# Attention and two feed-forward layers on one core: loads kept off the first two rows of maxima, the second copy of Q on ScalarE for two pairs, and another order around them

## The chip, the core and the metric

The kernel runs on one core of a Trainium2 chip. The core has five engines that run on their own and meet at semaphores: TensorE (PE) multiplies matrices, VectorE (DVE), ScalarE (ACT) and GpSimd (POOL) work on elements, and SyncE (SP) issues the DMAs, in the order in which they stand in its queue. The metric is the time of one execution in device microseconds; lower is better. Inputs and outputs lie in the chip's own memory (HBM).

## What is computed

```python
# attention over q, k, v of (4, 8, 576, 64) and s of (4, 8, 576)
scores = q @ k.T / sqrt(64)
cum = np.cumsum(np.maximum(s, 0.0), axis=-1)
scores = np.where(causal, -1e9, scores + np.minimum(cum[..., None, :] - cum[..., :, None], 0.0))
scores = scores - scores.max(-1, keepdims=True)
attn = np.exp(scores); attn = attn / (attn.sum(-1, keepdims=True) + 1e-9)
x = (attn @ v)                       # laid out as (2304, 512)
h = x @ moe_w_in;  x = (h - np.tanh(h)) @ moe_w_out           # 512 -> 2048 -> 512
h = x @ moe2_w_in; out = (h * clip(h + 3, 0, 6) / 6) @ moe2_w_out
```

## The kernel before

There are 32 heads, worked on two at a time as 16 *pairs* (p = 0 to 15). Every product is made of parts, a rounded high part and the rest as a low part, so that it comes out close to full precision. The attention stage runs over the pairs; the two feed-forward layers follow.

The program does not write its order out. It lists operations with an engine, an estimated duration, what they come after, the buffers that they take and a priority (PRIO), and `plan.schedule()` (L193 on) plays them in time: a free engine takes the ready operation of the smallest priority. The order that comes of it is what each engine and SP's queue then run. Afterwards the list MOVES puts four operations elsewhere by hand, and the table FILLS puts idle matmuls of zeros (L1354) on PE ahead of named operations, so many microseconds of them, but none ahead of an operation that stands behind the first pair's `pv`. The first zeros of all (L1369) run while the first loads are on their way.

For a pair these operations are made, by the names of the plan:

- `lq`, `lk` load Q and K of the pair (L490, 288 KB each; the first pair in halves, one per head). `lv` loads V (L598, 330 KB).
- `q1` makes the high part of Q (ACT, L466 and L468) and `kh` that of K (DVE, L477). `k2` is the second copy of the high part of K (ACT, L480), `q2` the second copy of that of Q, a DMA inside the core's memory (L279, `Q<-Q`, 288 KB). `ql` and `kl` are the low parts (POOL, L474 and L484). `cu` brings the cumulated s (L279, `K<-cdram`); it writes into the pair's K buffer, so it waits until the pair four before it has done with that buffer.
- `mx` are five products of high parts for the row maxima alone (PE, L531): `mx2_0` of pair 1 is the wide one, `mx2_1` to `mx2_4` take one bank each. `rd` reduces them (DVE, L540).
- `mf` turns the maxima into a row (DVE, L569 to L576), `mo` writes that row out (L279, `mdram<-xr`, 16 KB), and `mi` reads it back into the pair's Q buffer (L279, `Q<-mdram`). The maxima so enter the next product as one more row of it. `mo` and `mi` of a pair are what is called *a row of maxima under way* here. The first pair has two of them, one per head.
- `st` are the scores of a head in four chunks (PE, L633), `ex` their exponentials (ACT, L636), and `pv` the product with V and the sums of a pair (PE, L666 and L677). A chunk waits for a free PSUM bank; a bank of `mx` is free when its `rd` has read it, a bank of `st` when its `ex` has. `ov` (ACT, L701) empties the banks of `pv`.

Operations are named by the head that ends the pair: `mx4` and `rd4` are of pair 2, `st0` and `st1` of the heads of pair 0, `pv1` of pair 0.

The loads of later pairs wait for rows of maxima by this line, and those of V by the next one:

```python
[cm] if p == 1 else first_mo[:1] if p == 2 else first_mo[1:2] if p else []      # lq, lk
first_mo[1:2] if p else first_mo[:1]                                            # lv
```

`first_mo` is the list of all `mo`, in the order of the pairs, so that `first_mo[0]` and `first_mo[1]` are the two of pair 0.

Of the kernel before, what the change touches and what calls it, by code (L numbers as in the profile page):

```python
# [14 lines left out]
AF = mybir.ActivationFunctionType  # L15
# [17 lines left out]
FILLS = {"mx1_0": 0.9, "mx2_1": 3.0, "st0_0": 0.9, "mx4_1": 2.4, "st1_0": 0.5, "pv1_3": 1.5}  # L33
# [35 lines left out]
KDMA = ()  # L69
TINY, HUGE = (float(np.array([b], np.uint32).view(np.float32)[0]) for b in (0x38000000, 0x47F00000))  # L70
# [9 lines left out]
PRIO = {  # L80
# [3 lines left out]
}  # L84
# [46 lines left out]
class Plan:  # L131
    LAT = {"PE": 0.30, "ACT": 0.05, "DVE": 0.09, "POOL": 0.09, "V": 0.0}
    DMA_US, DMA_KB_US, ISSUE = 1.6, 220.0, 0.55
# [126 lines left out]
def kernel(  # L260
# [10 lines left out]
    nc = tc.nc  # L271
    plan = Plan()
# [43 lines left out]
    def r(b):  # L316
        return late[b.t] if isinstance(b.t, str) else b.t
# [125 lines left out]
    first_mf, first_mo = [], []  # L443
# [6 lines left out]
    def heads(p):  # L450
# [10 lines left out]
        for i, a in enumerate(parts):  # L461
# [26 lines left out]
            def ld(x, a=a):  # L488
                dst = r(tq)[x * D : (x + 1) * D, a].rearrange("p a s -> p (a s)")
                nc.sync.dma_start(dst, (q, k)[x][p][:, a.start * S : a.stop * S])  # L490

            lq, lk = (plan.dma(
                lambda x=x, ld=ld: ld(x), 147 * n, [cm] if p == 1 else first_mo[:1] if p == 2 else first_mo[1:2] if p else [], [tq], t + PRIO["lq"], name=f"l{'qk'[x]}{p}"
# [8 lines left out]
            oq2.append(plan.dma(q2, 147 * n, [oq1[-1], a2], [b1, b2], t + PRIO["q2"], name=f"q2_{p}"))  # L502
# [60 lines left out]
        for i, a in enumerate(parts):  # L563
# [27 lines left out]
            u = t0 + PRIO["mf"] if p else lead + a.start  # L591
# [843 lines left out]
```

## Time and profile before

| | |
|---|---|
| runs of the kernel, us | 947.81, 944.92, 949.15; median 947.81 |
| the profiled execution: its time, us | 944.47 |
| its span in the profile, us | 942.7 |
| PE busy | 931.3 us, 99% |
| DVE / ACT / POOL busy | 662.9 / 467.3 / 159.3 us |

The profile is of one execution of its own. A time counts some 1.8 us more than the span, which runs from the first to the last instruction. PE's busy time includes the matmuls of zeros. Times in the rows below are microseconds from the span's start.

### The profile page before, as it was taken

The page shows a single profiled execution, that of the slowest core. Times are in us where ns is not written, and L with a number is a line of the kernel's source. Part 1 is how long each engine was busy: PE and PEld are TensorE (multiplying, and loading weights), DVE is VectorE, ACT ScalarE, POOL GpSimd, SP SyncE. Part 2 cuts the span into 40 slices and gives each one's busy share as a digit, 9 for nine tenths or more (in the row PEclk, how much of TensorE's full clock was granted, in tenths as well). Part 3 has the DMA queues.
Part 4 walks back from the last instruction along what each step waited for, and adds up shares of the span by engine and source line. Part 5 has one row for each costly group of instructions (what it writes and reads, how often), then busy time and mean ns, then how long its engine had stood idle before and what let it go on. Part 6 is the DMA issues. An engine that isn't in the chain of part 4 may idle for free.

```text
span 942.7 us, 18003 instructions
## 1 busy us (share of the span) xinstructions
PE 931.3 (99%) x7112; PEld 839.0 (89%) x7112; DVE 662.9 (70%) x1059; ACT 467.3 (50%) x720; POOL 159.3 (17%) x113
## 2 busy tenths in 40 slices
PE   8999999999999999999999999999999999999998
PEld 5888888788788889988888888999999999999997
DVE  7798897889985776676577641848767477674763
ACT  7577777655443444444344333544545344454441
POOL 7446756500000000022332321000000000000000
PEclk9999999999999999999999999999999999999999
DMA  5666876777235445564546862766887668776762
GB/s 156 170 180 176 235 197 182 229 286 233 89 121 220 179 185 217 202 202 156 216 153 223 262 218 78 261 214 222 267 276 242 212 221 267 274 245 216 223 223 92
DMA packets 69793, 193.75 MB, mean 206 GB/s; under 512 B 11856, under 2 KB 20656, under 8 KB 68428
## 3 DMA queue, kind: packets, MB, share of 16 engines
q1 hardware_dynamic: 69708, 192.59, 63.0%
q8 instruction: 56, 0.92, 0.4%
q14 instruction: 29, 0.24, 0.1%
HBM read 143.74 MB, written 44.09 MB: 199 GB/s over the span
## 4 chain that ended last, share of the span: by engine, by line
PE 91%; DVE 5%; POOL 1%; DMA 1%; issue 1%; ACT 1%; SPq 0%; DVEq 0%; POOLq 0%; ACTq 0%
PE bank L903 21%; PE bank L934 20%; PE pair L1271 19%; PE pair L1195 18%; PE bank L633 5%; PE bank L666 3%; DVE xr L540 2%; PE bank L677 2%; PE bank L531 1%; PE wide L531 1%; DMA Q<-Q 1%; PE bank L1354 1%; DVE xr L572 1%; DVE K L477 0%; POOL K L484 0%
## 5 line engine op out<-in xcount | busy, mean ns | idle before, releaser
L934 PE MATMUL bank<-gg,w 128*128 128x512 f32 (+1 forms) x960 | 234.4, 368 | 0.5 <-ACT gg L922 0.5
L903 PE MATMUL bank<-xx,w 128*128 128x512 f32 (+1 forms) x960 | 233.4, 368 | 0.0
L934 PEld LDWEIGHTS bank<-gg,w 128*128 128x128 f32 x960 | 170.4, 188 | 30.6 <-ACT gg L922 0.9
L903 PEld LDWEIGHTS bank<-xx,w 128*128 128x128 f32 x960 | 170.4, 189 | 30.2 <-issue 0.2
L1195 PE MATMUL pair<-op_w,w 128*128 128x384 f32 x648 | 117.9, 335 | 0.2
L1195 PEld LDWEIGHTS pair<-op_w,w 128*128 128x128 f32 x648 | 112.4, 188 | 1.2 <-DVE g L918 0.6
L914 ACT ACTIVATE g<-bank 128x512 f32<-128x512 f32 (+1 forms) x80 | 44.4, 555 | 136.9 <-PE bank L903 66.3
L924 POOL TENSOR_TENSOR gg<-g,gg 128x512 fp32r<-128x512 f32 x32 | 48.3, 1510 | 343.8 <-ACT gg L922 246.6
L918 DVE TENSOR_TENSOR g<-bank,g 128x512 f32<-128x512 f32 (+1 forms) x80 | 50.9, 636 | 73.5 <-ACT g L914 72.6
L1271 PE MATMUL pair<-w,op_W 128*128 128x256 f32 x774 | 97.8, 283 | 0.0
L1271 PEld LDWEIGHTS pair<-w,op_W 128*128 128x128 f32 x774 | 95.4, 192 | 0.0
L922 ACT ACTIVATE gg<-g 128x512 fp32r<-128x512 f32 (+1 forms) x80 | 47.0, 588 | 49.4 <-DVE g L918 27.4
L633 PE MATMUL bank<-Q,K 128*128 128x320 f32 (+9 forms) x384 | 65.8, 313 | 1.8 <-DMA Q<-Q 0.9
L636 ACT ACTIVATE pt<-bank 128x512 f32<-128x512 f32 (+2 forms) x128 | 59.1, 508 | 17.1 <-PE bank L633 12.0
L633 PEld LDWEIGHTS bank<-Q,K 128*128 128x128 f32 (+3 forms) x384 | 56.2, 186 | 8.1 <-issue 2.5
L1271 PE MATMUL pair<-w,op_B 128*128 128x256 f32 x486 | 62.7, 283 | 0.0
L1271 PEld LDWEIGHTS pair<-w,op_B 128*128 128x128 f32 x486 | 60.5, 192 | 0.0
L540 DVE CUSTOM_DVE_ANT_0 xr<-bank,xr 128x512 bf16<-128x512 f32 (+3 forms) x96 | 49.0, 510 | 14.5 <-PE bank L531 3.8
L474 POOL TENSOR_TENSOR Q<-tq,Q 64x1152 fp32r<-64x1152 f32 (+1 forms) x17 | 43.0, 2530 | 46.5 <-PE bank L531 22.2
L666 PE MATMUL bank<-pt,vf 128*32 128x192 f32 (+3 forms) x1152 | 46.7, 315 | 0.0
L484 POOL TENSOR_TENSOR K<-tq,K 64x1152 fp32r<-64x1152 f32 (+1 forms) x17 | 42.8, 2522 | 10.9 <-ACT Q L468 3.7
L666 PEld LDWEIGHTS bank<-pt,vf 128*32 128x32 f32 x1152 | 32.1, 110 | 11.0 <-DVE xr L540 0.6
(322 smaller groups left out, 1347.2 us busy)
## 6 DMA issues: line engine op xcount, KB each, us to landing
w<-wdram SPq DMA_DIRECT2D x149, 512.0 KB
wdram<-cv SPq DMA_DIRECT2D x56, 512.0 KB
raw_c<-in_w_dram SPq DMA_DIRECT2D x11, 1024.0 KB
raw_b<-in_w_dram SPq DMA_DIRECT2D x11, 1024.0 KB
raw_a<-in_w_dram SPq DMA_DIRECT2D x12, 512.0 KB
vf<-in_v_dram SPq DMA_DIRECT2D x16, 330.0 KB
rb<-rdram SPq DMA_DIRECT2D x32, 144.0 KB
xdram<-xb SPq DMA_DIRECT2D x16, 288.0 KB
```

Source lines behind the costliest of these rows:

```text
L540: nc.vector.tensor_tensor_reduce(out=junk[0:rr, 0:w], in0=r(b)[0:rr, col : col + w], in1=maskB[:, 0:w] if hh < 0 else maskA[0:rr, m0 : m0 ...
L633: nc.tensor.matmul(o, w, x, start=(i == 0), stop=(i == len(mms) - 1), skip_group_check=True)
L636: nc.scalar.activation(r(pt), r(b)[:, 0 : CW[c]], AF.Exp, scale=0.125)
L666: nc.tensor.matmul(r((wide_b, rest_b)[far])[32 * i : 32 * i + 32, oc : oc + n], r(vf)[:, j, hh, d0 : d0 + 32], r(pts[hh][c])[:, col : col ...
L903: nc.tensor.matmul(r(ps)[:, 0:w], wt[:, c, :], x(c)[:, 0:w], start=(part == 0 and c == 0), stop=(part == 2 and c == NCC - 1),)
L914: nc.scalar.activation(r(g)[:, 0:w], r(ps)[:, 0:w], AF.Tanh)
L918: nc.vector.tensor_sub(x, r(ps)[:, 0:w], x)
L922: gho = plan.op("ACT", vec_us(w, 1.2, 205), lambda: nc.scalar.activation(r(gh)[:, 0:w], r(g)[:, 0:w], AF.Copy), [m, to_gg], [g, gh], base)
L924: glo = plan.op("DVE" if beside else "POOL", vec_us(w, 0.96, 155) if beside else vec_us(w, 0.44, 160), lambda: (nc.vector if beside else n ...
L934: nc.tensor.matmul(r(acc[e])[:, 0:w], a[:, es], bb[:, 0:w], start=f, stop=l)
L1195: nc.tensor.matmul(bank(k)[:, l], w[hw][:, l, kc], r(x)[:, hx, kc], start=(i in (1, 5, 2) and j == 0 and kc == 0), stop=(j == 2 and kc == ...
L1271: nc.tensor.matmul(r(c[k])[:, m * 256 : (m + 1) * 256], r(x)[:, hx, l, m * P : (m + 1) * P], w[hw][:, l], start=(i == order[chain_first[k] ...
```

## The change

Five things are changed.

- `lq2`, `lk2` get a fixed early priority, the loads of Q and K of pair 3 and later wait for `first_mo[2]`, the row of maxima of pair 1, in place of that of pair 0's second head; V of pair 0 waits for that second head's row and V of the later pairs for pair 1's `mi`; `q2` of pair 1 waits for the second row of pair 0 as well.
- For pairs 2 and 3 (QACT) `q2` is no DMA but an ACTIVATE on ACT that reads Q where it was loaded.
- `mf`, `mo` and `mi` of pair 1 get a priority ahead of all else.
- The priorities of the whole attention stage (PRIO) and the assumed DMA rate are other numbers, so the plan comes out in another order.
- FILLS has other lengths and places, and the conversion of the weights may begin after the scores of head 3 in place of head 1.

```diff
-FILLS = {"mx1_0": 0.9, "mx2_1": 3.0, "st0_0": 0.9, "mx4_1": 2.4, "st1_0": 0.5, "pv1_3": 1.5}
+FILLS = {"mx1_0": 0.9, "mx2_1": 4.4, "mx4_1": 1.2, "pv1_3": 0.7, "st3_0": 0.7}
...
+QACT = (2, 3)
...
-    ... "rd": 29.37,
+    ... "rd": 103.23,
...
-                ..., first_mo[:1] if p == 2 else first_mo[1:2] if p else [], [tq], t + PRIO["lq"], ...
+                ..., first_mo[:1] if p == 2 else first_mo[2:3] if p else [], [tq], lead + 2 if p == 2 else t + PRIO["lq"], ...
...
-            oq2.append(plan.dma(q2, 147 * n, [oq1[-1], a2], [b1, b2], t + PRIO["q2"], name=f"q2_{p}"))
+            if p in QACT:
+                oq2.append(plan.op("ACT", act, lambda a=a: nc.scalar.activation(r(b2)[0][0:64, a], r(tq)[0:64, a], AF.Copy), [lq, a2], [b2, tq], t + PRIO["k2"] + 1, name=f"q2_{p}"))
+            else:
+                oq2.append(plan.dma(q2, 147 * n, [oq1[-1], a2] + first_mo[1:2] * (p == 1), [b1, b2], lead + 5 if p == 1 else t + PRIO["q2"], name=f"q2_{p}"))
...
-            u = t0 + PRIO["mf"] if p else lead + a.start
+            u = t0 + PRIO["mf"] if p > 1 else lead + a.start - 100 * p
...
+            first_mi.append(omi[-1])
-        lv = plan.dma(..., first_mo[1:2] if p else first_mo[:1], [vf], t0 + PRIO["lv"], name=f"lv{p}")
+        lv = plan.dma(..., first_mi[2:3] if p else first_mo[1:2], [vf], t0 + PRIO["lv"] if p else lead + 3, name=f"lv{p}")
...
-                fc, [part], PRIO["conv"] + 2 * fc + part, [st_done[1][0]], rawp, wyp)
+                fc, [part], PRIO["conv"] + 2 * fc + part, [st_done[3][0]], rawp, wyp)
```

What it moves is seen at three places. Line numbers of the changed kernel are up to five higher. The first place is SP's queue from the `cu2` load on, before:

```order
L279 DMA K_2_103<-cdram 2x2x576
L279 DMA mdram<-xr 128x32
L279 DMA Q_1_110<-Q_1_99 64x2x576
L598 DMA vf_112<-in_v_dram 128x660
L279 DMA Q_0_96<-mdram 2x20x32
L490 DMA tq<-in_q_dram 64x1152
L490 DMA tq<-in_k_dram 64x1152
L279 DMA K_3_106<-cdram 2x2x576
L279 DMA mdram<-xr 128x32
L598 DMA vf_113<-in_v_dram 128x660
L598 DMA vf_114<-in_v_dram 128x660
L279 DMA Q_0_96<-mdram 2x20x32
```

and the same place now, as far as the loads of pair 3:

```order
L280 DMA mdram<-xr 128x32
L280 DMA Q_0_96<-mdram 2x20x32
L491 DMA tq<-in_q_dram 64x1152
L491 DMA tq<-in_k_dram 64x1152
L280 DMA K_3_106<-cdram 2x2x576
L280 DMA mdram<-xr 128x32
L280 DMA Q_0_96<-mdram 2x20x32
L603 DMA vf_112<-in_v_dram 128x660
L280 DMA Q_1_110<-Q_1_99 64x2x576
L280 DMA mdram<-xr 128x32
L280 DMA K_0_97<-cdram 2x2x576
L280 DMA Q_1_99<-mdram 2x40x32
```

The copy `q2` of pair 1 (`Q_1_110<-Q_1_99`) and `lv0` (`vf_112`) have gone from between `mo` and `mi` of the first head to behind both rows, `lv1` and `lv2` from between `mo` and `mi` of the second head to further back; `lq2` and `lk2` (`tq`) still stand between the first `mi` and the second `mo`. Behind the last row shown come `lq3` and `lk3`, which before stood right behind the twelve rows of before; now `cu4` (`K_0_97`) and the row of pair 1 are ahead of them.

The second place is DVE and ACT around the first head's scores. On DVE the end of `rd2`, before:

```order
L540 ISA xr<-bank_66,xr 128x128
L540 ISA xr 128x1
L540 ISA xr<-wide,xr 128x576
L540 ISA xr 128x1
L540 ISA xr<-wide,xr 128x384
L540 ISA xr 128x1
L569 COPY xr<-xr 64x1
L572 TENSOR_SCALAR xr<-xr 128x10
L573 SCALAR_TENSOR_TENSOR xr<-xr 128x10
L576 STREAM_TRANSPOSE xr<-xr 128x32
L477 CAST K_2_103<-tq 64x2x576
```

and now:

```order
L544 ISA xr<-bank_66,xr 128x128
L544 ISA xr 128x1
L478 CAST K_2_103<-tq 64x2x576
L544 ISA xr<-wide,xr 128x576
L544 ISA xr 128x1
L544 ISA xr<-wide,xr 128x384
L544 ISA xr 128x1
L544 ISA xr<-bank_73,xr 128x512
L544 ISA xr 128x1
L544 ISA xr<-bank_71,xr 128x512
L544 ISA xr 128x1
L573 COPY xr<-xr 64x1
```

`kh2` (the CAST) now stands ahead of the wide reduction, and `mf1` (from the COPY on) behind the first two reductions of pair 2. On ACT from the second exponential of head 1 on, before:

```order
L636 ACTIVATE pt_1_119<-bank_73 128x320
L466 ACTIVATE Q_3_105<-tq 64x2x576
L468 ACTIVATE Q_3_107<-tq 64x64
L636 ACTIVATE pt_1_122<-bank_65 128x512
L636 ACTIVATE pt_1_125<-bank_70 128x512
L480 ACTIVATE K_0_109<-tq 64x2x576
L466 ACTIVATE Q_0_96<-tq 64x2x576
```

and now, from the third on:

```order
L641 ACTIVATE pt_1_122<-bank_73 128x512
L641 ACTIVATE pt_1_125<-bank_71 128x512
L481 ACTIVATE K_0_109<-tq 64x2x576
L504 ACTIVATE Q_0_108<-tq 64x1152
L467 ACTIVATE Q_3_105<-tq 64x2x576
L469 ACTIVATE Q_3_107<-tq 64x64
L641 ACTIVATE pt_2_117<-bank_65 128x256
L641 ACTIVATE pt_2_120<-bank_73 128x320
L706 ACTIVATE stage<-bank_70 128x288
L706 ACTIVATE xb_83<-bank_72 128x384
L641 ACTIVATE pt_2_123<-bank_71 128x512
L706 ACTIVATE xb_83<-bank_70 128x192
```

Before, `q1` of pair 3 (`Q_3_105`, `Q_3_107`) stood ahead of the last two exponentials of head 1. Now it stands behind them and behind the new copy `q2` of pair 2 (L504), and ahead of the first exponential of head 2; `q1` of pair 4 and then the last exponential of head 2, again from bank_71, follow the rows shown.

The third place is PE between the maxima of pair 14 and the scores of head 24, before:

```order
L531 MATMUL bank_65<-K_2_103,Q_2_102 128x384
L531 MATMUL bank_65<-K_2_103,Q_2_102 128x128
L633 MATMUL bank_66<-Q_0_108,K_0_109 128x256
L633 MATMUL bank_66<-Q_0_96,K_0_97 128x256
L633 LDWEIGHTS identb
L633 MATMUL bank_66<-maskT,identb 128x128
L633 MATMUL bank_70<-Q_0_108,K_0_109 128x320
L633 MATMUL bank_70<-Q_0_96,K_0_97 128x320
L666 MATMUL bank_73<-pt_1_116,vf_114 32x256 x2
```

and now:

```order
L535 MATMUL bank_66<-K_2_103,Q_2_102 128x384
L535 MATMUL bank_66<-K_2_103,Q_2_102 128x128
L671 MATMUL bank_71<-pt_1_116,vf_114 32x256 x2
L671 MATMUL bank_71<-pt_2_117,vf_114 32x256 x2
L671 MATMUL bank_71<-pt_1_119,vf_114 32x128 x2
```

The first two chunks of head 24 (`st24_0`, `st24_1`) stood ahead of `pv23` and now stand behind it. On PE at the start the rows of zeros now count 7, 38, 10 and 6 (ahead of `mx1_0`, `mx2_1`, `mx4_1` and `pv1`), before 7, 26, 7, 20, 4 and 13; the entry for `st3_0` puts none in.

## Rows read from the trace of the kernel before

**Rows 1.** The page, busy time of each engine, share of the span, instructions

```profile
PE 931.3 (99%) x7112; PEld 839.0 (89%) x7112; DVE 662.9 (70%) x1059; ACT 467.3 (50%) x720; POOL 159.3 (17%) x113
```

**Rows 2.** Waits of PE from 30.5 us on: in total, times, longest

```profile
PE bank L633 <- DMA Q<-Q: 0.9, 1, 0.9
PE bank L633 <- POOL K L484: 0.8, 1, 0.8
PE bank L934 <- ACT gg L922: 0.5, 1, 0.5
PE wide L531 <- ACT xb L701: 0.4, 1, 0.4
```

**Rows 3.** Timeline of PE: start, duration, what, [idle before, releaser]

```profile
11.27 3.01 PE L1354 MATMUL bank<-xr 128*128 128x256 bf16 x26
15.79 0.70 PE L531 MATMUL bank<-K,Q 66*128 66x512 f32 x2 [1.50 <-DVE K L477]
...
24.76 1.17 PE L531 MATMUL bank<-K,Q 66*128 66x512 f32 x6 [0.48 <-issue]
...
30.56 2.92 PE L666 MATMUL bank<-pt,vf 128*32 128x256 f32 x72
...
34.81 0.73 PE L531 MATMUL bank<-K,Q 66*128 66x512 f32 x2
...
36.72 0.45 PE L633 MATMUL bank<-Q,K 128*128 128x256 f32 x2
...
38.60 0.49 PE L633 MATMUL bank<-Q,K 128*128 128x256 f32 x2
...
42.87 2.92 PE L666 MATMUL bank<-pt,vf 128*32 128x256 f32 x72
```

**Rows 4.** Stretches: busy by engine, PE's granted clock, DMA share, GB/s

```profile
17.40:20.80 3.40, 3.40 (x17) 2.85 (x16) 2.87 (x12) 0.53 (x2) 2.67 (x2) 0.50 0.95 249
```

**Rows 5.** Timeline of DVE

```profile
17.90 0.67 DVE L540 CUSTOM_DVE_ANT_0 xr<-bank,xr 128x512 bf16<-128x512 f32 x1
21.66 0.76 DVE L540 CUSTOM_DVE_ANT_0 xr<-wide,xr 128x576 bf16<-128x576 f32 x1
23.90 0.76 DVE L477 CAST K<-tq 64x1152 fp32r<-64x1152 f32 x1
25.27 0.69 DVE L540 CUSTOM_DVE_ANT_0 xr<-bank,xr 128x512 bf16<-128x512 f32 x1 [0.61 <-PE bank L531]
30.48 0.15 DVE L569 COPY xr<-xr 64x1 f32<-64x1 f32 x1
47.84 0.76 DVE L477 CAST K<-tq 64x1152 fp32r<-64x1152 f32 x1
```

**Rows 6.** Timeline of SP's queue, issues

```profile
9.64 0.59 SPq L490 DMA_DIRECT2D tq<-in_k_dram  x1
...
13.69 0.36 SPq L279 DMA_DIRECT2D mdram<-xr  x1
...
15.53 0.79 SPq L279 DMA_DIRECT2D Q<-mdram  x1
16.95 0.59 SPq L490 DMA_DIRECT2D tq<-in_k_dram  x1
...
29.11 0.25 SPq L279 DMA_DIRECT2D K<-cdram  x1
```

**Rows 7.** Timeline of ACT

```profile
12.53 1.16 ACT L466 ACTIVATE Q<-tq 64x1152 fp32r<-64x1152 f32 x1 [1.19 <-DMA tq<-in_q_dram]
14.17 1.16 ACT L480 ACTIVATE K<-tq 64x1152 fp32r<-64x1152 f32 x1 [0.33 <-DMA tq<-in_k_dram]
28.33 1.15 ACT L466 ACTIVATE Q<-tq 64x1152 fp32r<-64x1152 f32 x1
29.53 1.06 ACT L636 ACTIVATE pt<-bank 128x512 f32<-128x512 f32 x2
```

**Rows 8.** The chain that ended last: start, duration, what

```profile
136.60 8.29 DMA Q<-Q
```

More of the change, by code (lines that the diff above doesn't have):

```diff
@@ L132 @@
     LAT = {"PE": 0.30, "ACT": 0.05, "DVE": 0.09, "POOL": 0.09, "V": 0.0}
-    DMA_US, DMA_KB_US, ISSUE = 1.6, 220.0, 0.55
+    DMA_US, DMA_KB_US, ISSUE = 1.6, 240.0, 0.55
     def __init__(self):
@@ L442 @@
     alloc_prev = [None, None]
-    first_mf, first_mo = [], []
+    first_mf, first_mo, first_mi = [], [], []
     filled = []
@@ L492, in heads @@
             lq, lk = (plan.dma(
-                lambda x=x, ld=ld: ld(x), 147 * n, [cm] if p == 1 else first_mo[:1] if p == 2 else first_mo[1:2] if p else [], [tq], t + PRIO["lq"], name=f"l{'qk'[x]}{p}"
+                lambda x=x, ld=ld: ld(x), 147 * n, [cm] if p == 1 else first_mo[:1] if p == 2 else first_mo[2:3] if p else [], [tq], lead + 2 if p == 2 else t + PRIO["lq"], name=f"l{'qk'[x]}{p}"
             ) for x in range(2))
@@ L596, in heads @@
             omi.append(plan.dma(mi, 5, [omo], [b1], u, name=f"mi{p}"))
-        lv = plan.dma(lambda: nc.sync.dma_start(r(vf).rearrange("p j a d -> p (j a d)"), v[p]), 338, first_mo[1:2] if p else first_mo[:1], [vf], t0 + PRIO["lv"], name=f"lv{p}")
+            first_mi.append(omi[-1])
+        lv = plan.dma(lambda: nc.sync.dma_start(r(vf).rearrange("p j a d -> p (j a d)"), v[p]), 338, first_mi[2:3] if p else first_mo[1:2], [vf], t0 + PRIO["lv"] if p else lead + 3, name=f"lv{p}")
         k2s.append(ok2[-1])
```

6 rows, old and new, of the table PRIO are left out of this document.

## The prediction

> **What bounds the kernel now.** The page comes first [rows 1]: PE is busy for 99% of the span. That figure hides two things. Zeros count as busy, and all 77 of them stand in the first 31 us. So the second view is PE's waits from 30.5 us on [rows 2]: in all that is left PE waits 2.6 us. From the first `pv` on, the kernel is a queue of matmuls without gaps, and a change of order can win there no more than those 2.6 us. What is left to win lies ahead of `pv1` at 30.56 [rows 3].
>
> The third view is PE's timeline up to there [rows 3]. The useful work ahead of `pv1` is five sets of maxima or their halves and two heads. One set takes 1.91 us (34.81 to 36.72) and one head 1.88 us (36.72 to 38.60) at full clock. The rest is zeros and waiting: `mx2` waits 1.50 us for `kh1`, `mx4` begins at 24.76, after 0.48 us of idle, as soon as `kh2` is done (23.90 + 0.76) [rows 3, 5]. So `kh2` on DVE set `mx4`, and `mx4`, `st1` and the exponentials behind it set `pv1`: the last two of head 1 end at 29.53 + 1.06 = 30.59 [rows 7]. The chain through the start is DVE's, not that of the rows of maxima alone.
>
> **The start, step by step.** Zeros ahead of `mx2` go from 26 to 38. 26 take 3.01 us [rows 3], so 38 take 4.40 us and end at 15.67, just as `kh1` is done; the 1.50 us of idle go. Behind that idle the granted clock stood at 0.50 for 3.4 us [rows 4], so `mx2` and the first chunks of `st0` ran at the lower level (1.2 GHz). Now `mx2` ends at 15.79 + 1.91 = 17.7.
>
> `st0` needs the first row. Its `mo` was issued at 13.69, and `mi` at 15.53 did not wait [rows 6], so 1.84 us bound such a small transfer when nothing big is ahead of it; it was the big copies between the two that came ahead of `mi`. Now `mi` is issued at 15.5 and lands by 17.4, and `st0` begins at 17.7, with no zeros ahead of it. Its third chunk takes bank_72, which the first reduction of pair 1 (17.90 + 0.67) frees at 18.7 [rows 5], so `st0` ends at 19.9.
>
> `kh2` moves ahead of the wide reduction, which began at 21.66 [rows 5]: it ends at 22.42 and `mx4` begins at 22.5, 2.25 us sooner. That needs `lk2` by 21.66. `lk1` was issued at 9.64 and awaited at 14.17, 4.53 us [rows 6, 7]; `lk2`, issued at 16.95 as before, lands by 21.5. It is close, but the loads ahead of it have gone. The wide part of `mx4` then waits for the wide reduction (from 22.42 on, some 1.4 us by its 0.76 us for 576 of 960 columns), so `mx4` ends at 24.9 and `st1` at 26.8. The second row still has `lq2` and `lk2` ahead of it; behind 21.5 and twice 1.84 would be 25.2 at the very latest, against a need at 24.9, and since `mo` was issued at 18.1, its own time runs beside theirs. I count it at nothing.
>
> With `q1` of pair 3 (1.15 us and a short one, at 28.33 [rows 7]) gone from between the exponentials, the last one ends 0.8 us behind `st1`, and **`pv1` begins at 27.8 and not at 30.56: -2.75 us.**
>
> **What is given back.** `lq3` and `lk3` now stand behind `cu4` and the row of pair 1. `cu4` was issued at 29.11, when `st1` was done [rows 6]; it now goes at 26.9. `mf1` ends at 26.4 (the two reductions of pair 2 ahead of it and 0.85 us of its own, behind 23.85; 0.85 is what the 2.24 us from 21.66 to 23.90 leave beside the wide reduction [rows 5]), its `mo` takes 1.84 us, `mi` 0.79 us of issue, so `lk3` is issued at 29.65. By `lk1`'s 4.53 us it lands at 34.2; with nothing but `lq3` ahead of it sooner. I take 33.5. `kh3` then ends at 34.25. PE, at 27.8 + 4.25 for `pv1` (30.56 to 34.81) + 1.26 for three chunks of head 2 = 33.3, **waits 1.05 us** for it ahead of `mx6`. Before, this load was long there.
>
> A rule of the Trainium skill bears on this: DMA: Bandwidth & Descriptors, section "Queues, rings and completion order", says that each DMA engine takes its descriptors in the order of its ring. By that rule `lk3` waits for `lq3` alone, 0.59 MB in all at the 249 GB/s of [rows 4], and lands at about 33.0, which would make the sum 0.5 us better.
>
> ACT: `lq1` was there 1.64 us ahead of `lk1` [rows 7], so `lq3` comes at 31.9 and `q1` of pair 3 holds ACT from then to 33.3, ahead of the exponentials of head 2. `q1` of pair 4 stands ahead of the last of these, and `st3`'s third chunk takes the same bank_71: ACT's work from 33.3 on sums to 4.4 us, so that chunk begins at 38.0 and PE **waits 0.5 us**. The two copies on ACT themselves (some 1.16 us each, as `q1`) lie beside `pv1` and `pv3`, where ACT waits for PE anyway; without that cover each would cost as much.
>
> DVE: five reductions take 5.2 us (25.27 to 30.48 [rows 5]). Four of them now stand ahead of `kh4`: from 34.9, when the first product of `mx6` is there, 4.2 us and 0.76 us give 39.9. PE, ready for `mx8` at 39.2, **waits 0.7 us**. So `pv3` begins at 41.85. Before it was 42.87 [rows 3] with a quarter of a head (0.46 us) done that now comes later, 42.41 like for like. **Of 2.75 us, 0.55 us are left.** DVE says the same at `kh5`: 39.9 + 1.0 + 5.2 + two `mf` of 0.85 + 0.76 = 48.6, where before it ended at 47.84 + 0.76 = 48.6 [rows 5]. DVE hardly gains there, and PE's lead is some half microsecond of scores done beforehand.
>
> **Later.** The wait of 0.9 us for `Q<-Q` [rows 2] is the copy `q2` of pair 12: 8.29 us from issue to landing [rows 8]. Its first user, `st24_0`, stood ahead of `pv23` and now stands behind it, 4.25 us later, so **the wait goes: -0.9 us**. Those of 0.8, 0.5 and 0.4 I leave as they are: bounds 0 and twice as long. Converting the weights later costs nothing, since from 190 us on PE has no wait for it in [rows 2] and the last part was done before.
>
> **The sum**: -2.75 + 1.05 + 0.5 + 0.7 = -0.5, and -0.9 from the later wait: -1.5 us with the rounding. The profiled execution takes 944.47 us, so 943.0 for one like it. It lies 3.3 us under the median of the runs, 947.81, and the times to come are of that kind: 946.3.
>
> **Rivals.** *The clock falls again* (chance 0.16). Ten zeros behind `st0` last 1.16 us, to 21.05, and `mx4` comes at 22.5: 1.45 us of idle, where 1.50 us were followed by 3.4 us at 0.50 [rows 3, 4]; the idle of 0.48 was not. Then half of 3.4 us, 1.7 us, is lost in `mx4` and `st1`. The row of pair 1 does not wait for that, so `lk3` is only 0.45 us later and the waits behind it shrink; DVE's `kh4` ends at 40.5, and 0.65 us remain: 947.0. The skill's page TensorE: Matmul & The Clock Gate, Part 1, speaks for it: the array is throttled by default and activity lifts that. By that rule alone the sum would be -0.85.
>
> *DVE takes it all* (0.17). It is the engine that PE waits for at 24.76 and, by time, at 48.6. If it loses the half microsecond too, and another wait takes the place of that at `st24`, nothing is won: 947.8. This is also the case where the change does what it says and it doesn't matter, since rows of maxima were not what PE waited for.
>
> *Slower* (0.13). `lk3` was issued early before and its time was hidden; now it is on the path. If it lands as late as the `Q<-Q` of 8.29 us, at 37.95, `mx6` is 4.45 us later than counted, and the sum is +2.95: 950.8. It decides from 1.5 us on, that is a landing behind 35.0. Against it: that copy had a stretch full of other transfers ahead of it.
>
> *All of it stays* (0.14). `lk3` and ACT are in time and no new wait arises: -2.75 and -0.9, 944.1.
>
> My forecast has 0.40. The range is 943.2 to 950.8: the fast case and 0.9 us more for the other old waits, and the slow case. A measurement of this kernel tells some 0.5%, 4.7 us, from no change, and no case reaches that far alone: faster 0.06, same 0.89, slower 0.05.
>
> **What would show it.** Right: `pv1` at 27 to 28.5 us; PE's clock full from 17 to 21 us; a wait of PE for `kh3` (L478) near 33 us and one ahead of `mx8`; no wait for `Q<-Q` near 145 us; `pv3` within a microsecond of 41.9. Wrong: `pv1` behind 29.5 would mean that `lk2` or the second row was late; a wait of over 3 us at `mx6` the slow rival; no waits between 32 and 42 us the fast one. A change of over 5 us could only come from the feed-forward layers, where I see PE without waits and the same work.

## The result and the profile after

| | before | after |
|---|---|---|
| runs, us: median (lowest to highest) | 947.36 (944.92 to 949.15), 6 runs | 957.27 (952.52 to 964.59), 6 runs |
| ratio of the times, 95% interval | | 1.011 (1.0067 to 1.0155) |
| mean granted clock of PE, six runs of after | | 0.982 to 0.992 |
| profiled execution: time, span, us | 944.47, 942.7 | 964.59, 962.8 |

The changed kernel is about 10 us, 1.1%, slower. The forecast was 946.3 us and the range ended at 950.8: the prediction was wrong. The execution that was profiled is the slowest of the six, so its rows show the loss enlarged.

Of the page, the busy time of each engine in the changed kernel, and then PE's waits from 30.5 us on (in total, times, longest):

```profile
PE 944.6 (98%) x7096; PEld 847.5 (88%) x7096; DVE 661.9 (69%) x1059; ACT 468.7 (49%) x722; POOL 158.1 (16%) x113
```

```profile
PE bank L638 <- DMA Q<-mdram: 2.7, 1, 2.7
PE bank L535 <- ACT xb L706: 2.5, 1, 2.5
PE wide L535 <- DVE K L478: 1.7, 1, 1.7
PE bank L638 <- ACT xb L706: 0.8, 1, 0.8
PE wide L535 <- DVE xr L577: 0.7, 1, 0.7
```

PE is 13.3 us longer busy than in [rows 1] with 16 matmuls of zeros fewer, and its waits have grown from one of 0.9 us [rows 2] to two of over 2.5 us. Longer busy on the same work fits a slower clock, which the stretches below show. PE's timeline of the start:

```profile
22.41 1.17 PE L535 MATMUL bank<-K,Q 66*128 66x512 f32 x6 [1.17 <-ACT pt L641]
...
27.45 2.92 PE L671 MATMUL bank<-pt,vf 128*32 128x256 f32 x72
...
35.79 0.47 PE L535 MATMUL bank<-K,Q 66*128 66x512 f32 x1 [2.55 <-ACT xb L706]
...
46.50 4.86 PE L671 MATMUL bank<-pt,vf 128*32 128x256 f32 x72
```

`pv1` begins at 27.45, 3.1 us sooner than in [rows 3]. Then `mx6` waits 2.55 us, and the next `pv` takes 4.86 us for what took 2.92. The releaser named ahead of `mx6`, the last `xb` of ACT, frees a bank; `kh3` on DVE ended within 0.04 us of it. Timelines of DVE, SP's queue and ACT:

```profile
34.93 0.76 DVE L478 CAST K<-tq 64x1152 fp32r<-64x1152 f32 x1 [4.51 <-DMA tq<-in_k_dram]
```

```profile
26.29 0.32 SPq L280 DMA_DIRECT2D mdram<-xr  x1
26.77 0.25 SPq L280 DMA_DIRECT2D K<-cdram  x1
27.74 0.66 SPq L280 DMA_DIRECT2D Q<-mdram  x1
28.50 0.52 SPq L491 DMA_DIRECT2D tq<-in_q_dram  x1
29.08 0.59 SPq L491 DMA_DIRECT2D tq<-in_k_dram  x1
29.76 0.54 SPq L491 DMA_DIRECT2D tq<-in_q_dram  x1
30.36 1.05 SPq L603 DMA_DIRECT2D vf<-in_v_dram  x2
```

```profile
32.39 1.16 ACT L467 ACTIVATE Q<-tq 64x1152 fp32r<-64x1152 f32 x1 [2.51 <-DMA tq<-in_q_dram]
...
35.32 0.32 ACT L706 ACTIVATE xb<-bank 128x192 f32<-128x192 f32 x1
```

`lk3` was issued at 29.08 behind the row of pair 1, as foreseen, but landed at 34.93, 5.85 us later, and `kh3` ended at 35.69. `lq3` landed at 32.39, and ACT, which waited 2.5 us for it ahead of two exponentials and the emptying of `pv`'s banks, was done with the last bank at 35.64. Two chains from the same held loads end together, and `mx6` began at 35.79. The stretches of both kernels (busy time by engine, PE's granted clock, share of the DMA engines' time, GB/s; before first) show what else was under way:

```profile
15.00:20.00 5.00, 4.21 (x22) 3.51 (x22) 4.40 (x16) 2.54 (x3) 2.31 (x4) 0.74 0.86 219
20.00:25.00 5.00, 4.52 (x35) 3.94 (x34) 4.12 (x16) 3.09 (x6) 3.31 (x2) 0.92 0.78 228
25.00:30.00 5.00, 5.00 (x39) 4.41 (x39) 4.00 (x15) 2.35 (x5) 1.03 (x1) 1.00 0.99 231
30.00:35.00 5.00, 5.00 (x127) 3.93 (x126) 3.40 (x8) 3.72 (x7) 2.92 (x2) 1.00 0.80 242
```

```profile
15.00:20.00 5.00, 4.65 (x32) 3.75 (x31) 4.40 (x16) 3.45 (x5) 2.31 (x4) 1.00 0.51 121
20.00:25.00 5.00, 3.56 (x25) 2.87 (x22) 4.37 (x16) 2.27 (x4) 3.31 (x2) 1.00 0.36 102
25.00:30.00 5.00, 5.00 (x89) 4.03 (x91) 4.39 (x20) 4.31 (x6) 2.67 (x2) 1.00 0.26 51
30.00:35.00 5.00, 3.24 (x70) 2.65 (x58) 0.45 (x3) 2.61 (x7) 2.64 (x1) 1.00 0.98 248
...
36.85:50.50 13.65, 13.65 (x94) 10.90 (x97) 9.80 (x37) 8.07 (x13) 5.27 (x2) 0.50 0.69 192
149.50:163.10 13.60, 13.60 (x104) 10.67 (x106) 9.26 (x23) 6.17 (x10) 7.54 (x3) 0.50 0.56 152
190.50:197.30 6.80, 6.58 (x58) 4.78 (x61) 1.61 (x3) 3.14 (x6) 1.14 (x1) 0.50 0.85 296
```

From 15 to 30 us the kernel before moves 5 us x (219 + 228 + 231 GB/s) = 3.4 MB, the changed one 1.4 MB. The 2.0 MB held back come afterwards, when the DMA engines are full. And three times, behind the waits ahead of `mx6`, of pair 14's maxima (1.7 us) and of head 30 (2.7 us), the granted clock stood at 0.50, for 34.05 us in all, where before it was 3.4 us [rows 4].

That accounts for the profiled execution. Half of the half-clock time is lost: (34.05 - 3.4) / 2 = 15.3 us. PE's idle time from its first to its last matmul is 13.5 us, and was 6.7: 6.8 us. 16 zeros fewer, of 0.116 us each (3.01 us for 26 in [rows 3]), give back 1.9. The sum is 20.2, and the spans differ by 20.1. All of it lies in the attention stage: the last product of scores ends at 202.17 us, before at 181.28; what follows takes 760.6 us, before 761.4.

### The profile page after: what moved, and what is told of

It reads as the page before. It is cut to its first block, busy times and chain, and to the rows that moved or that the text cites. A ratio compares the mean times of both kernels' runs of the same rounds, so it can differ in the third digit from the quotient of the medians.

```text
span 962.8 us, 17954 instructions
## 1 busy us (share of the span) xinstructions
PE 944.6 (98%) x7096; PEld 847.5 (88%) x7096; DVE 661.9 (69%) x1059; ACT 468.7 (49%) x722; POOL 158.1 (16%) x113
## 4 chain that ended last, share of the span: by engine, by line
PE 92%; DMA 4%; DVE 3%; ACT 1%; issue 1%; SPq 0%; DVEq 0%; ACTq 0%
PE bank L908 21%; PE bank L939 20%; PE pair L1200 18%; PE pair L1276 18%; PE bank L638 6%; PE bank L671 4%; PE wide L535 2%; PE bank L535 1%; PE bank L682 1%; DVE xr L544 1%; DMA w<-wdram 1%; DMA raw_a<-in_w_dram 1%; DMA Q<-mdram 1%; PE bank L1359 1%; DMA mdram<-xr 1%
## 5 line engine op out<-in xcount | busy, mean ns | idle before, releaser
L1276 PE MATMUL pair<-w,op_W 128*128 128x256 f32 x918 | 115.1, 283 | 0.0
L1276 PEld LDWEIGHTS pair<-w,op_W 128*128 128x128 f32 x918 | 112.8, 192 | 0.0
L638 PE MATMUL bank<-Q,K 128*128 128x320 f32 (+9 forms) x384 | 72.2, 331 | 4.2 <-DMA Q<-mdram 2.7
L638 PEld LDWEIGHTS bank<-Q,K 128*128 128x128 f32 (+3 forms) x384 | 61.0, 200 | 11.9 <-issue 3.2
L671 PE MATMUL bank<-pt,vf 128*32 128x192 f32 (+3 forms) x1152 | 52.4, 341 | 0.0
L671 PEld LDWEIGHTS bank<-pt,vf 128*32 128x32 f32 x1152 | 34.7, 119 | 14.4 <-issue 4.0
L1276 PE MATMUL pair<-w,op_B 128*128 128x256 f32 x342 | 44.2, 283 | 0.0
L1276 PEld LDWEIGHTS pair<-w,op_B 128*128 128x128 f32 x342 | 42.5, 192 | 0.1
```

The costliest lines, as they stand in the source:

```text
L638: nc.tensor.matmul(o, w, x, start=(i == 0), stop=(i == len(mms) - 1), skip_group_check=True)
L671: nc.tensor.matmul(r((wide_b, rest_b)[far])[32 * i : 32 * i + 32, oc : oc + n], r(vf)[:, j, hh, d0 : d0 + 32], r(pts[hh][c])[:, col : col ...
L1276: nc.tensor.matmul(r(c[k])[:, m * 256 : (m + 1) * 256], r(x)[:, hx, l, m * P : (m + 1) * P], w[hw][:, l], start=(i == order[chain_first[k] ...
```

## The experiments

Each time is a median, with the number of runs and the ratio to the kernel before on the same chip and its 95% interval. Theory 1 was at first: a late load and the falls of the clock behind waits. Theory 2: many small waits, the clock a by-product. Theory 3: the order of the later pairs. A fall is a stretch at a granted clock of 0.50. A clock given for a run is its mean granted clock, 1.000 being full speed. Only one execution of each kernel was profiled; of the others the time and the mean clock are known.

### The early wait

**K of pair 3 early**, in the changed kernel; SP issues it right behind `q2` of pair 1:

```diff
+MOVES += [("lq3", 0, "q2_1", 0), ("lk3", 0, "lq3", 0)]
```

> The changed kernel with the loads of Q and K of pair 3 put back ahead of the row of pair 1 on SP's queue (issued at about 23.4 and 24.0 us instead of 28.5 and 29.1); all else as it is. Theory 1 (the late load and the clock): PE's wait of 2.55 us ahead of the maxima of pair 3 goes, the clock does not fall to 0.50 at 37 us, and the time falls by 2.5 + 6.8 us, from 957.3 to about 948. Theory 2 (many small waits of the new order, the clock costs little): 954 to 955, the wait alone. Theory 3 (the order of the later pairs, with its waits at 147 and 188 us, makes the loss): 954 to 957.

The wait ahead of `mx6` went and the time hardly did: the clock fell behind the 1.16 us ahead of `mx4`, which it had not done in the profile after, and again near 117, 148 and 189 us. PE's timeline and the first of these stretches:

```profile
22.43 1.17 PE L535 MATMUL bank<-K,Q 66*128 66x512 f32 x6 [1.16 <-ACT pt L641]
```

```profile
25.10:31.90 6.80, 6.80 (x56) 5.00 (x59) 5.82 (x23) 4.94 (x7) 3.58 (x2) 0.50 0.54 112
```

956.02, 6 runs, 1.011 (1.0078 to 1.0142). The 948 of theory 1 is missed by 8 us; one late load alone is not the cause.

**Zeros in the wait ahead of `mx6`** of the changed kernel (22 of them; FILLS now allows that one place behind `pv1`):

```diff
-... "st3_0": 0.7}
+... "mx6_1": 2.6}
```

> The changed kernel with 22 matmuls of zeros (2.55 us at full clock) on PE ahead of the first product of the maxima of pair 3, so that PE is busy while it waits there; the wait for the load itself stays. Theory 1: the maxima begin at the same 35.8 us, the clock stays at 1.00 through 37 to 50 us, and the time falls by the 6.8 us that the half clock cost, to about 950.5. Theory 2: the wait stays and so does the time, 956 to 957. Theory 3: the same, 956 to 957.

No fall at 37 us, but falls at 24.7, 45.2, 120, 151 and 189 us: 958.8, 6 runs, 1.0119 (1.0091 to 1.0147). It is no test of the zeros: behind the fall at 24.7 us PE was so late in the profiled execution that `kh3` was done at 35.20, ahead of the zeros (36.28 to 38.60), and they covered no wait.

**The late load alone**, in the kernel before:

```diff
+MOVES += [("lq3", 0, "mi1", 0), ("lk3", 0, "lq3", 0)]
```

> The kernel before with one thing of the change: its loads of Q and K of pair 3 stand behind the row of pair 1 on SP's queue (issued at about 30.2 and 30.8 us instead of 22.8 and 23.4). Theory 1: PE waits 1.5 to 3 us ahead of the maxima of pair 3 (34.8 us), the clock falls behind it for some 13 us, and the time rises by 8 to 10 us, from 947.4 to about 956. Theory 2: it rises by the wait alone, 949 to 950.5. Theory 3: 947.5 to 950.5 as well.

PE's timeline and the stretch behind it:

```profile
38.46 1.22 PE L531 MATMUL bank<-K,Q 66*128 66x512 f32 x2 [3.55 <-DVE K L477]
```

```profile
37.80:54.90 17.10, 16.44 (x79) 14.08 (x83) 11.17 (x39) 6.88 (x12) 7.90 (x3) 0.50 0.32 80
```

953.44, 10 runs, 1.0054 (1.0028 to 1.008). The runs are of two kinds: four at a mean clock of 0.995 or 0.996 take 947.5 to 949.6 us, five at 0.984 to 0.989 take 954.4 to 956.6, and one at 0.993 lies between. The profiled one is of the second kind; whether PE waited as long in the first isn't known.

**The same late load with 28 zeros in its wait** (`"mx6_1": 3.3` in FILLS, at that place alone):

> The kernel before with the load of K of pair 3 issued late, as in the run that did so (wait of 3.55 us ahead of mx6, half clock for 17 us, 953.4 us), and 28 zeros, 3.2 us at full clock, put into that wait and nowhere else. It prices the clock alone, since the load comes as late. Theory 1: the wait shrinks to under 1 us, no half clock behind it, every run at a mean clock of 0.995 or more, and 947.5 to 950 us. Theory 2: the late load itself costs it, so the time stays at 952 to 954, whatever the clock.

```profile
37.33 3.23 PE L1354 MATMUL bank<-xr 128*128 128x256 bf16 x28
40.32 0.71 PE L531 MATMUL bank<-K,Q 66*128 66x512 f32 x2
```

```profile
36.00:60.00 24.00, 23.58 (x328) 20.34 (x324) 18.25 (x58) 14.12 (x29) 10.03 (x4) 1.00 0.51 131
```

`mx6` follows the zeros without a gap and the clock stays at 1.00: 949.97, 12 runs, 1.0028 (1.0011 to 1.0044). The median is 3.5 us lower, but the two intervals overlap, and the load was less late for PE in the run profiled here: a fall of 10.2 us behind the old wait at 14 us put the whole start 2.5 us later, `lk3` took 4.45 us from issue and not 6.83, and `kh3` was done at 38.5, 1.2 us behind the first of the zeros. So this run points to a price of the fall by itself and doesn't measure it; the clocks of the runs, 0.993 to 0.998, reach lower than expected.

**The early stretch mended**: K of pair 3 early, and 20 zeros ahead of `mx4` in place of 10:

> The changed kernel with its early stretch mended by hand and its later order as it is: the loads of Q and K of pair 3 early, as in the first experiment, and 20 zeros in place of 10 ahead of mx4. Early: pv1 at 27.5 to 28 us, no wait over 0.6 us and no half clock up to 60 us. What is left against the kernel before is the order of the later pairs at 240 KB/us: waits of some 1.5 us near 114, 2.2 near 146 and 2.7 near 187 us, and the half clock behind them. Theory 1 as it stands now, early and late losses of like size: 950 to 954. If the late order costs nothing: 945 to 948. If it costs everything: 955 to 957, as in the first experiment.

954.59, 7 runs, 1.0067 (1.0042 to 1.0093). The waits left are 0.7 us at 39, 1.8 at 112, 0.7 at 145 and 2.1 and 1.7 near 178 us, the falls 3.4 us at 19, 6.8 at 114 and 6.8 at 179. Up to `pv1`, at 28.37, 2.2 us are still won; the loss comes behind it, most of it from 112 us on.

### The start of the change in the old order

**Start by hand** in the kernel before: the loads behind the first rows, `kh2` early, 38 zeros ahead of `mx2`; its later order stays.

```diff
+MOVES += [("q2_1", 0, "mi0", 1), ("lv0", 0, "mi0", 1), ("lv2", 0, "mo1", 0), ("lv1", 0, "mo1", 0), ("rd2_0", 0, "kh2", 0),
+          ("mf1", 0, "rd2_0", 0), ("kl1", 0, "kh2", 0), ("q1_3", 0, "ex1_3", 0)]
+FILLS = {"mx1_0": 0.9, "mx2_1": 4.4, "mx4_1": 1.2, "pv1_3": 0.7}
```

> The kernel before with the good part of the change alone: the copy of Q of pair 1 and V of pairs 0 to 2 behind the rows of maxima, the high part of K of pair 2 ahead of the wide reduction, Q of pair 3 on ScalarE behind the exponentials of head 1, the changed kernel's zeros; the loads of pair 3 stay ahead of the row of pair 1, and all later pairs keep their old order. Theory 1: the first product with V begins at about 27.5 us instead of 30.6, no fall of the clock behind it, and the time falls by 2 to 3 us to about 945. If the loads of pair 3 are late even there, a wait and a fall of the clock cost 7 us and it ends near 952. Theory 2 and 3: 944.5 to 946 too, since the later order is that of before.

953.33, 12 runs, 1.0051 (1.0025 to 1.0077). Three of the twelve ran at a clock of 0.996 and took 945.2 to 947.0 us; the others, at 0.986 to 0.991, took 951.7 to 955.8. The profiled execution is of the others: its clock fell for 6.8 us at 26.1, `pv1` began at 30.12 and not near 27.5, and behind a wait of 1.92 us ahead of the scores of head 2 the clock fell for 13.7 us more. At a clock of 0.996 the kernel before took 947.0 and 947.4 us on the same chip: from so few runs, about a microsecond of the start's gain is there when the clock holds, and the whole of it isn't shown.

**The same with PE held by 20 zeros ahead of `mx4`**, the row of pair 1 ahead of the loads of pair 4 and of V, and ACT's first step on the weights (`awl`) behind `ov` of pair 0, which are these moves beside others:

```diff
+("mf1", 0, "rd4_2", 0), ("mo1", 0, "mf1", 0), ("mi1", 0, "mo1", 0), ("lk4", 0, "mi1", 0), ("lq4", 0, "mi1", 0),
+("lv2", 0, "lk4", 0), ("lv1", 0, "lk4", 0), ("kh4", 0, "rd6_3", 0), ("q1_4", 0, "ov0_1", 0),
+("awl0_0", 0, "ov0_1", 0)
```

> The kernel before with the good part of the change, as in the fourth run, and with the waits that this run showed taken away: the row of pair 1 ahead of the loads of pair 4, of V of pairs 1 and 2 and of the first weights, these loads' users on ScalarE and VectorE placed behind what is ready sooner, and 20 zeros in place of 10 ahead of the maxima of pair 2, so that PE is not idle there. All pairs from pair 4 on as before. Theory 1 (each idle of PE of a microsecond or more can bring the clock down, and that is most of the loss): no idle over 0.7 us from 10 to 140 us, clock 0.995 or more in nearly all runs, first product with V at 27.5 us, time 944 to 945, 2 to 3 us under before. Theory 2 (the clock is a by-product): 944 to 945 too, but with runs at 0.989 that are no slower. Theory 3 (the order of the later pairs makes the loss): 944 to 945.

PE had no idle above 0.34 us from 10.3 to 36.2 us and `pv1` began at 27.88. Then ACT waited:

```profile
39.96 0.66 ACT L825 ACTIVATE wy<-raw_a 128x512 f32<-128x512 f32 x1 [6.67 <-DMA raw_a<-in_w_dram]
```

The weights, issued at 32.54 behind two loads of Q and K and two of V, stand on ACT ahead of head 2's exponentials: PE waited 7.3 us and the clock fell for 13.7. 956.29, 5 runs, 1.0103 (1.0082 to 1.0123): not a test of the start, since the order made by hand put a new wait in.

**The same, weights later**, with the first steps on them on ACT and DVE (`awl` and `bwl`):

```diff
+("wl0_1", 0, "lk5", 0), ("wl0_0", 0, "lk5", 0), ("mi2", 0, "lv3", 0), ("q1_4", 0, "ex2_3", 0),
+("awl0_0", 0, "ex3_3", 0), ("awl0_1", 0, "awl0_0", 0), ("bwl0_0", 0, "kh5", 0)
```

> The start of the change without its later order, and mended where the run with the held start failed: two weight loads go behind the loads of pair 5, their first ScalarE and VectorE steps behind head 3's exponentials and kh5, q1 of pair 4 behind head 2's exponentials, and the row of pair 2 comes back ahead of the loads of pair 5. Theory 1 (a late load and clock falls): pv1 near 27.9 us, no PE wait over 1 us between 10 and 60 us, no half clock there, and 943.5 to 946 us, ratio 0.996 to 0.999: what the start wins is kept. Theory 2 (many small waits take it, the clock is a by-product): the waits go on behind 36 us, DVE is at kh5 no sooner than 48 us, and 946 to 948. Theory 3 (the order of the later pairs costs the ten microseconds): no loss here, 944 to 947.5.

The wait moved. PE's waits from 35 to 60 us, and ACT's timeline:

```profile
PE wide L531 <- ACT Q L466: 5.2, 1, 5.2
PE bank L633 <- DMA sdram<-stage: 2.0, 1, 2.0
```

```profile
52.53 0.66 ACT L825 ACTIVATE wy<-raw_a 128x512 f32<-128x512 f32 x1 [12.87 <-DMA raw_a<-in_w_dram]
```

The row of pair 2, issued at 34.42, took until 40.49, and the weights, issued at 43.70, until 52.51. 957.52, 6 runs, 1.0103 (1.0082 to 1.0125). No run made the whole of the start's gain stay.

### The later waits

**Zeros in the changed kernel's five longest waits** (21 to 24 in each, 12 and 18 in two):

```diff
+"mx4_1": 2.5, "mx6_1": 2.6, "st17_2": 1.4, "mx28_0": 2.1, "st30_0": 2.8
```

> The changed kernel with zeros on PE in all its long waits (21 in place of 10 ahead of the maxima of pair 2, 22 ahead of those of pair 3, 12 ahead of the third chunk of head 17, 18 ahead of the wide maxima of pair 14, 24 ahead of head 30); nothing else is moved, and what PE waits for comes as late as before. Theory 1: the granted clock of the runs rises from 0.982 to 0.992 to 0.996 or more, and the time falls from 957.3 to 947 to 949, that is to what the runs of the changed kernel give when the time lost to the clock is taken off. Theory 2: the waits stay, 956 to 957. Theory 3: the same as theory 2, since the later order is untouched.

953.37, 6 runs, 1.0077 (1.0055 to 1.01), clocks 0.993 to 1.000, one fall of 3.4 us in the profile. Theory 1's 947 to 949 is missed. By the medians it is 4 us faster than after, by the ratios some 3 us, and the intervals overlap, so the size is uncertain. The 87 zeros that it has more last 10.1 us and take the place of 7.2 us of PE's idle time (13.5 us, now 6.3), so they outlast the waits by some 3 us; without that more would have come back. What stays is the waits: its profile has as much half clock as the kernel before (3.4 us) and as little idle time (6.7 us there), but 71 zeros more, 8.2 us, and its span is 7.9 us longer.

**Planned at the old rate**, 220 KB/us, in the changed kernel:

```diff
-    DMA_US, DMA_KB_US, ISSUE = 1.6, 240.0, 0.55
+    DMA_US, DMA_KB_US, ISSUE = 1.6, 220.0, 0.55
```

> The changed kernel with one number undone: the plan counts with 220 KB per us for the DMAs, as before, in place of 240, and is made anew with it, so the order moves in many places. It tests where the later waits come from. If the rate is behind them (ScalarE waits in its order for loads of weights that the plan expects too soon, 12.5 us of such waits from 45 to 200 us against 4 us before), ScalarE's waits for weights fall to 4 to 6 us, PE's waits behind 100 us fall under 3 us, the clock's falls at 147 and 188 us go, and the time is 949 to 952. If it is the priorities, they stay and the time is 955 to 959.

Behind 100 us PE waits 2.4 us, and of the falls there one of 3.4 us is left, but the new plan waits 3.4 us at 20 and 1.6 at 43 us: 954.71, 6 runs, 1.0084 (1.0055 to 1.0113). With 29 and 13 zeros in those two:

> The changed kernel planned at 220 KB/us, whose later waits were 2.4 us in all, with zeros in its two early waits: 29 ahead of the first chunk of st1 (wait 3.37 us) and 13 ahead of mx8 (1.64 us). The loads come no sooner than in the run at 220 KB/us (954.7 us). Theory 1 (late loads, and the clock that falls behind their waits): half clock of 13.6 us goes, worth 6.8 us, of which the zeros give back 1 to 2, so 948 to 951, with every run's mean clock at 0.994 or more. Theory 2 (the waits themselves cost it): 953 to 955. Theory 3 (order of the later pairs): with that order mended already, the time is again that of the run at 220.

953.64, 11 runs, 1.0066 (1.0044 to 1.0089), clocks 0.993 to 0.999. Theory 1's 948 to 951 is missed: with zeros the clock stays higher, but what PE waits for comes no sooner.

### One part at a time, planned anew

**The held loads undone in the changed kernel**, for Q and K of pairs 3 and later:

```diff
-                ... first_mo[:1] if p == 2 else first_mo[2:3] if p else [] ...
+                ... first_mo[:1] if p == 2 else first_mo[1:2] if p else [] ...
```

> The changed kernel with one part undone: Q and K of pairs 3 and later wait again for the second row of pair 0, not for that of pair 1; all else, the 240 KB/us too, stays, and the plan is made anew. Theory 1 (held loads early, the plan's rate late, each half): DMA busy again from 20 to 30 us, no wait of 2.5 us for K of pair 3, but ScalarE's waits for weights behind 60 us (12.5 us) and PE's waits behind 90 us stay: 950 to 955. If the held loads are all of it: 946 to 949. If the order of the later pairs is all: 955 to 958.

954.41, 6 runs, 1.0074 (1.0051 to 1.0098). **Hold and rate undone:**

> As the run before, with the plan at 220 KB/us as well: both suspected parts undone, while the second copy of Q on ScalarE, the fixed priorities, the new numbers of PRIO, FILLS and the later weights stay. Theory 1: neither the early nor the late waits, 945 to 949. If it stays above 952, the loss is not in those two parts but in any order that PRIO's new numbers give.

956.21, 6 runs, 1.0098 (1.0075 to 1.0122). Theory 1 fell here: without both suspected parts the loss is whole, though in another form, since this plan waits 3.2 us ahead of the scores of head 1, as that at 220 KB/us did. **The rate alone, 240, in the kernel before:**

> The kernel before with the assumed rate alone changed, 240 KB/us in place of 220, and planned anew. Theory 1: loads are expected sooner than they land, so ScalarE waits for weights and PE for what stands behind it, 2 to 5 us of waits behind 30 us and falls of the clock: 949 to 954. If the rate is innocent: 946 to 949.

952.17, 12 runs, 1.0063 (1.0041 to 1.0086). **The held loads alone in the kernel before:**

> The kernel before with the held loads alone: Q and K of pairs 3 and later wait for the row of pair 1, planned anew at 220 KB/us with the old numbers. Theory 1: the DMA engines idle from 20 to 28 us and are full behind that, K of pair 3 lands at 35 us or later, PE waits 1 to 4 us for it, the clock falls behind: 950 to 955. If the hold is innocent: 946 to 949.

952.66, 8 runs, 1.0061 (1.0034 to 1.0088). ACT's wait for weights between 45 and 200 us, as the views of waits of five kernels give it (before, after, rate alone, hold alone, both undone):

```profile
ACT wy L825 <- DMA raw_a<-in_w_dram: 4.1, 4, 1.7
```

```profile
ACT wy L830 <- DMA raw_a<-in_w_dram: 12.5, 6, 3.6
```

```profile
ACT wy L825 <- DMA raw_a<-in_w_dram: 10.7, 6, 4.0
```

```profile
ACT wy L825 <- DMA raw_a<-in_w_dram: 4.6, 4, 1.5
```

```profile
ACT wy L830 <- DMA raw_a<-in_w_dram: 9.9, 5, 3.5
```

The waits at 240 KB/us fit a plan that expects the weights too soon and puts ACT's steps on them ahead of exponentials; but the new numbers of PRIO bring 9.9 us of it at 220 as well. All four orders have PE waits of up to 2.1 us at other places, between 3.5 and 5.6 us in all from 30 us to the last scores (before 2.2), and a fall of 6.8 to 10.2 us behind at least one. In the two made from the kernel before, `pv1` also begins 1.8 and 2.0 us later. No part is guilty alone: each edit makes another order of the whole stage, and each of these orders has more waits than the one before. A rival stays untested: that the order of the kernel before is an uncommonly good one, and that any new plan, whatever the edit, would lose as much.

### Zeros alone, in the order of before

**38 zeros ahead of `mx2`**, one part of the change by itself:

> The kernel before with one part of the change alone: 38 zeros ahead of mx2 in place of 26. Both theories: the idle of 1.5 us and the half clock of 3.4 us behind it at 17 us go. Theory 1: pv1 stays near 30.5 since kh2 sets it, so 946.5 to 948, ratio 0.999 to 1.001: a fall of the clock in a stretch that waits for something else costs nothing. If a fall costs half its length anywhere, 945.5 or below.

947.6, 12 runs, 1.0002 (0.9984 to 1.0019). The idle at 14 us is covered, and the wait moves to `mx4`, 1.78 us, with a fall of 6.8 us behind it in the profile. **34 ahead of `mx4` as well:**

```diff
-... "mx2_1": 3.0, ... "mx4_1": 2.4, ...
+... "mx2_1": 4.4, ... "mx4_1": 3.95, ...
```

> The kernel before in its own order, with zeros alone changed: 38 in place of 26 ahead of mx2 and 34 in place of 20 ahead of mx4, where the run with 38 ahead of mx2 waited 1.78 us (23.00 to 24.78) and the clock then fell for 6.8 us. If waits and the falls behind them are the price (the theory as it now stands): no half clock between 14 and 40 us, mean clocks 0.996 or more, 945 to 947, ratio 0.997 to 1.000. If the order alone is: 947 to 948, no change.

945.19, 12 runs, 0.9985 (0.9972 to 0.9997). **And 10 ahead of head 24**, `"st24_0": 1.2`:

> As the run before, with 10 zeros more ahead of the first chunk of head 24, where the kernel before waits for the second copy of Q of pair 12 (0.9 us in its profile, 1.76 us in another run of the same order). If waits and falls are the price: 944.5 to 946.5, mean clocks 0.997 or more, ratio 0.996 to 0.999. If the zeros run past the end of the wait, up to 1 us is lost again and it equals the run before.

```profile
10.00:30.00 20.00, 19.03 (x150) 16.61 (x151) 17.02 (x61) 11.46 (x18) 10.66 (x18) 1.00 0.79 200
30.00:200.00 170.00, 167.88 (x2585) 141.40 (x2584) 140.35 (x362) 122.37 (x240) 91.20 (x41) 1.00 0.73 206
```

944.51, 12 runs, 0.9978 (0.9965 to 0.9992), clocks 0.999 to 1.000, 943.6 to 946.5 us. `pv1` begins at 30.56 as in [rows 3], so no step of the work up to there is sooner; PE is only kept busy in three places. In this run and in the one before it the clock is what changed, and their intervals lie under 1. It is faster than both kernels, by 2.6 and by 12.8 us, and its runs spread over 2.9 us, those of the kernel before beside them over 5.9.

## Why the prediction was wrong, point by point

**The start** was right: `mx4` at 22.41 (22.5), `pv1` at 27.45 (27.8), clock 1.00 from 15 to 30 us in the profiled execution. That the clock held there was luck: PE waited 1.17 us ahead of `mx4`, and in two of the four profiled executions with this start and this wait (K of pair 3 early; zeros ahead of `mx6`) it fell at 25 us. The prediction had given that 0.16.

**K of pair 3** was mis-sized: it was to land at 33.5, at 34.2 at the latest, and landed at 34.93. The issue was right (29.08 for 29.65); the load took 5.85 us where `lk1` had taken 4.53. The loads issued behind it are not the reason. In the run with zeros ahead of `mx6` the same loads follow it in the same order, and it took 4.35 us:

```profile
30.09 0.59 SPq L491 DMA_DIRECT2D tq<-in_k_dram  x1
```

```profile
34.44 0.76 DVE L478 CAST K<-tq 64x1152 fp32r<-64x1152 f32 x1 [3.31 <-DMA tq<-in_k_dram]
```

The trace shows what was late. The semaphore of a load is raised in sixteen steps; fifteen of those of `lk3` came from 33.04 to 33.40 us, the last at 34.91. By the Trainium skill's rule of ring order that the prediction weighed (DMA: Bandwidth & Descriptors, "Queues, rings and completion order") `lk3` had to wait for `lq3` alone and to land at 33.0; fifteen of its sixteen steps agree with that within 0.4 us. In the profile after, one 16 KB packet of another queue was under way from 31.42 to 32.66 us, by the list of DMA queues from 28.5 to 35 us (packets, MB, share of 16 engines):

```profile
q8 instruction: 1, 0.02, 1.2%
```

The run with zeros in all five waits has such a packet there too and the same late last step (5.78 us from issue), the run with zeros ahead of `mx6` has neither. That this packet held up the last step is likely and not shown, since the records don't say which of the DMA engines carried it. The term was 1.05 and measured 2.55. Without the late step ACT would have held `mx6` as long: `lq3` came at 32.39 (31.9 foreseen), and that `mx6` needs a bank which ACT empties behind it was not in the sum.

**The price of a wait** is the step that failed most. Each wait that I counted, 1.05, 0.5 and 0.7 us, was priced at its own length. The clock was a rival at one place, ahead of `mx4`, with 1.7 us, after the one fall of 3.4 us in [rows 4]. Falls took 3.4 to 17.1 us here, so up to 1.7 to 8.6 us each where PE is busy throughout. It shows from run to run: the six times of after go with their clocks, 0.992 at 952.5 and 954.2, 0.987 at 956.7 and 957.8, 0.984 and 0.982 at 959.1 and 964.6. With medians of 0.987 and 0.995 (the kernel before in its 23 runs beside the first experiments) the clock takes some 12.4 and 4.7 us, an estimate from those means times the span; that is 7.7 of the 9.9 us. It is a rough one: between 0.984 and 0.982 it would give 2 us, and those two runs differ by 5.5, so waits differ from run to run too. That falls cost time by themselves is shown by the last two runs (2.0 and 2.6 us won, with intervals under 1); that they are not all of the loss is shown by the zeros in all five waits.

**The waits of 0.5 and 0.7 us** ahead of `st3`'s third chunk and `mx8` did not come: PE, at half clock, was late itself. `pv3` began at 46.50 and not at 41.85: 1.5 us by the wait, and 4.8 us by the clock, half of the 9.65 us from 36.85 on, less the 1.2 us of waits that did not come and the 0.35 us that `pv1` was sooner.

**"Those of 0.8, 0.5 and 0.4 I leave as they are"** failed. The wait for `q2` of pair 12 went, as said, but 0.7, 0.8, 1.7 and 2.7 us came at 94, 118, 147 and 188 us. A new order was read only where it was argued, up to 50 us. The same holds for weights that were to cost nothing: ACT waits 12.5 us for them, 4.1 before.

**"Over 5 us could only come from the feed-forward layers"** failed: these took 760.6 us, as before (761.4).

**The rivals.** *Slower* named the right load and a price of 2.95 us from a landing behind 35.0; the load stayed just short of it and cost more, because of the clock. *The clock falls again* had the mechanism without its size. Together, several times over, they are what happened, and I had given each one place. What stays open is which of PRIO's numbers makes the later waits, and whether any order keeps the start's 2.75 us; none of these did.

## What to carry to other kernels

Where PE is the bound and waits for nothing, a change of order is judged by the waits that it makes anywhere in the stage, and each wait of half a microsecond or more is priced with the clock that may fall behind it: its length, and at some chance 1.7 to 8.6 us more, by the falls seen here. Compare mean granted clocks run by run before looking for a cause in the order, and try covering idle places with zeros before moving work: here that won 2.6 us, and the new order lost ten. A zero that outlasts the wait is lost time, so its number has to be fitted to the wait. Holding loads back for a small urgent transfer moves their bytes into a later stretch; sum the megabytes of both stretches against the rate that the trace shows.

## What was not expected of the hardware

A fall did not end soon with PE busy: 13.65 us at 0.50 with PE busy for all 13.65 us of it. The twenty profiled executions have 39 falls in the attention stage. Behind which wait one comes can't be told from its length: behind 1.16 us ahead of `mx4` the clock fell for 6.8 us in one run, and not behind 1.17 us at the same place in another; behind 0.60 us ahead of `mx8` it fell for 3.4 us (zeros ahead of `mx6`), and behind 1.76 us ahead of head 24 it did not (the late load with zeros). In the early stretch mended it fell at 18.75 us although PE had not waited for more than 0.36 us since 11.2. The Trainium skill, TensorE: Matmul & The Clock Gate, Part 1, says that throttled is the default and activity lifts it; 38 of the 39 falls stand closely behind a wait of PE of 0.5 us or more, or within it, which agrees with that, and the length of the falls is what these rows add.
